# Exponential in PSUM, gate in the result copies, division at the end, three score units a pair, a new order

## The chip, the cores and the metric

The kernel runs on one core of a Trainium2 chip. Its engines work side by side, each through its own instructions in order, and wait for one another by semaphores: PE (TensorE, matrix products and transposes), DVE (VectorE), ACT (ScalarE), POOL (GpSimd) and SP (SyncE, which here only issues DMAs). SBUF is the working memory; PSUM takes what PE writes and can be read and written by DVE and ACT. The metric is the device time of one execution in microseconds.

## What is computed

Eight batches (`b`) of eight heads, 576 rows of 64. First a layer of attention: a causal softmax (`local`), and a linear memory that is read with a feature map `phi`; a gate `g` per head mixes both. Then a soft mixture of experts on the joined heads, with two softmaxes over the same logits: over all rows for each slot (dispatch `d`) and over the 32 slots for each row (combine `c`).

```
scores = q @ k.T / 8, causal;  a = exp(scores - max);  a /= a.sum + 1e-9;  local = a @ v
phi(x) = where(x > 0, x, exp(x) - 1) + 1
mem_out = (phi(q) @ M_prev) / (phi(q) @ z_prev + 1e-6)
x = g * mem_out + (1 - g) * local
logits = x @ moe_phi                                # 4608 rows x 32 slots
d = softmax over rows, c = softmax over slots
slot_in = d.T @ x;  slot_out[e] = relu(slot_in[e] @ w1[e]) @ w2[e];  out = c @ slot_out
```

## The kernel before, in words

**Attention part.** The 64 (batch, head) problems go two heads at a time: `n` counts 32 pairs. The first 64 rows of each head are taken out and done apart by the *aux* steps (names that begin with `a`, 16 units of two batches), so that a pair has 512 rows in four tiles `i` of 128, with 192, 320, 448 and 576 keys. For each pair the steps are, by the names of their functions `op_...`:

- `ldq`, `ldv` load. `qhi`, `qlo`, `khi`, `klo` split q and k into two parts (`X`, `K`); most of this is on POOL.
- `qp1` makes q + 1 on POOL (L375), `qexp` makes exp(q) on ACT (L379) into the SBUF tile `e`, and `qphi` joins them on DVE into `f` = max(min(e, 1), q + 1) (L383). `ap1`, `aexp`, `aphi` do the same for aux units (`af`, `ae`, `pha`, L537).
- `s` makes the scores in PSUM (L392, six matmuls for each stretch of keys), in four units: `3a` and `3b` (288 keys each of tile 3), `2` (448) and `10` (320 and 192). `mx` takes the mask and the running minimum of the negated scores on DVE (L416), and `ex` the exponential with its sum on ACT (L424), the sum going to the tile `sum`.
- `t` transposes the weights on PE (L427), `te` copies them out of PSUM (to `at`; L307 is the copy on ACT, L310 that on DVE), `av` multiplies with v (L455) into `oa`, `oe` copies the result to `os`.
- `rs` (L476) multiplies the sums with a gate factor into `R`. `u` brings `os` and the memory product into PSUM (L427, L489), `dn` (L493, L496) makes the reciprocals in `R`, `mu` (L501) multiplies all four parts by `R` into `w`, and `ad` adds the two halves on POOL (L514) into the batch tile `x`. For aux units `adn` (L596 to L598), `amu`, `aad` do the same.

For each of nine groups `g` (eight batches and the aux rows) follow `x3` (transpose x), `x1` (logits), `x1l` (copy them to `lt`), `x1m` (three DVE steps, L649 to L652: the group's maximum, the running maximum `mrun`, its negative `nmn`), `x1e` (exponentials), `x1d` (`den`, L663), `x2` and `x2m`, `x2e`, `x2s` (the softmax over slots; `row_scale`, L695 to L698, sums, adds 1e-9, inverts and multiplies), `x4` and `x4a` (L711, slot sums into `acc`).

**PSUM.** The pool `psD` has three slots of two banks (0, 1, 2); each unit (`s`, `t`, `u`, `x3` and others) takes one by a number written in the order. `psO` is one bank for `oa`. `psM` is one bank with a single buffer (`misc`): the aux values, the logits and the slot sums share it.

**Order.** Nothing is scheduled at run time. `SEQ` is one long table of steps, `step@n:slot`; the program emits them in this order, and each engine runs its own in that order. `EV` gives the engine of each copy (`a`, `p`, `v`). `w@x` are loads of expert weights, 512 KB each: 19 into tiles that stay, 18 more into tiles that attention no longer needs; `WORD` lists them.

**Tail.** After the last pair a few small steps (`y4` to `y12`) finish the dispatch softmax. Then the experts (`f1`, `f1t`, `f2`) run while the other 27 weight tiles are reloaded on SP's queue, and `comb` multiplies each group's `cT` with the experts' output; of its four 256-column results two are copied by ACT and two by DVE in one instruction each, and written out.

Of the kernel before, what the change touches and what calls it, by code (L numbers as in the profile page):

```python
# [26 lines left out]
gate@0 la@0 ldq@1 ldv@1 la@1 khi@0 qhi@0 qp1@0 qlo@0 qexp@0 klo@0 qphi@0 s.3a@0:0 ldq@2 s.2@0:1 aexp@0 ap1@0 mx.3a.0@0  # L27
mx.3a.1@0 s.3b@0:2 mx.2.0@0 as@0:0 mx.3b.0@0 ex.2.0@0 khi@1 mx.3b.1@0 ex.3.0@0 mx.2.1@0 klo@1 s.10@0:2 ex.3.1@0 aphi@0
amx.0@0 amx.1@0 mx.1.0@0 ex.2.1@0 t.A@0:0 qhi@1 mx.0.0@0 mx.1.1@0 aex.0@0 t.B@0:1 qlo@1 mx.0.1@0 te.A0@0 te.A1@0
aex.1@0 te.B0@0 te.B1@0 at@0:0 qp1@1 te.Bq@0 s.3a@1:2 ate@0 ex.1.0@0 s.2@1:0 khi@2 mx.3a.0@1 ex.0.0@0 mx.3a.1@1  # L30
s.3b@1:1 ex.1.1@0 mx.2.0@1 klo@2 s.10@1:2 ex.0.1@0 mx.3b.0@1 ex.2.0@1 av.3@0 rs@0 mx.3b.1@1 ex.3.0@1 qhi@2 mx.2.1@1
av.2@0 ex.3.1@1 qlo@2 mx.1.0@1 mx.0.0@1 aav@0 ex.2.1@1 mx.1.1@1 t.C@0:0 mx.0.1@1 ap1@1 aoe@0 oe.1@0 qexp@1 t.B@1:2
te.C0@0 te.C1@0 au@0:1 ldq@3 te.Cq@0 te.B0@1 te.B1@1 t.A@1:0 te.Bq@1 la@2 adn@0 ex.1.0@1 u.1@0:2 amu@0 te.A0@1 qphi@1
aad@0 s.3a@2:1 te.A1@1 av.0@0 dn.1@0 ex.0.0@1 av.1@0 mu.1@0 ex.1.1@1 av.3@1 mx.3a.0@2 ad.1@0 oe.0@0 mx.3a.1@2 ex.0.1@1
khi@3 aexp@1 av.2@1 rs@1 qexp@2 aphi@1 klo@3 aexp@2 u.0@0:1 oe.1@1 t.C@1:2 dn.0@0 ldv@2 qhi@3 s.3b@2:0 mu.0@0 te.C0@1
w@0 mx.3b.0@2 s.2@2:1 ad.0@0 te.C1@1 te.Cq@1 mx.3b.1@2 ex.3.0@2 as@1:2 qlo@3 mx.2.0@2 x3.0@0:0 ex.3.1@2 mx.2.1@2
# [1020 lines left out]
```

## Time and profile before

| | us |
|---|---|
| median of 3 runs | 500.87 (499.87 to 505.47) |
| profiled execution | 504.95 |
| its span, first to last instruction | 503.2 |
| PE busy | 413.8 (82%) |
| DVE busy | 369.2 (73%) |
| ACT busy | 320.1 (64%) |
| POOL busy | 205.9 (41%) |

The page shares out 503.2 us. A busy time is the time in which an engine had an instruction under way; PE's matmuls overlap, so its share is no measure of how near it is to its best. The attention part runs to about 420 us, the tail from 432 us on. TensorE's clock has two levels, and the profile gives the granted clock as a share of the upper one.

### The profile page before, as it was taken

To read this page: it belongs to the slowest core of one execution; us is meant where nothing else is said; L and a number is where in the kernel's file an instruction comes from. 1 tells how busy PE (TensorE), PEld (TensorE's weight loads), DVE (VectorE), ACT (ScalarE), POOL (GpSimd) and SP (SyncE) were. 2 spreads that over 40 slices of the span, in tenths; PEclk is the share of its full clock that TensorE was granted. 3 is DMA by queue.
4 is the path that set the end of the run, shared out by engine and by line. 5 is a ranking of instruction groups with operands and counts; after the bars stand their busy time and mean duration, and the time that the engine had idled before them with its cause. 6 is when DMAs were issued, how large, how long until landed. Compare 5 with 4: busy or idle time off the path is not lost. (4 is left out here: it accounts for less than half of the span.)

```text
span 503.2 us, 20521 instructions
## 1 busy us (share of the span) xinstructions
PE 413.8 (82%) x8597; PEld 336.5 (67%) x8597; DVE 369.2 (73%) x1301; ACT 320.1 (64%) x986; POOL 205.9 (41%) x259
## 2 busy tenths in 40 slices
...
GB/s 336 62 193 141 160 149 150 147 162 153 132 157 141 82 216 148 142 171 165 114 136 90 173 122 92 91 91 46 137 175 100 184 393 90 87 388 408 397 373 232
DMA packets 30940, 87.12 MB, mean 173 GB/s; under 512 B 2816, under 2 KB 12288, under 8 KB 30848
## 3 DMA queue, kind: packets, MB, share of 16 engines
...
q14 instruction: 24, 0.20, 0.1%
q10 hardware_dynamic: 288, 0.08, 0.1%
...
## 5 line engine op out<-in xcount | busy, mean ns | idle before, releaser
L424 ACT ACTIVATE p<-p,nm 128x192 f32<-128x192 f32 (+3 forms) x256 | 155.3, 610 | 23.0 <-DVE nm L416 22.8
L392 PE MATMUL psD<-K,X 64*128 64x288 f32 (+3 forms) x960 | 103.1, 335 | 28.0 <-DVE w L501 5.2
L416 DVE CUSTOM_DVE_ANT_0 p<-psD,mk 128x192 f32<-128x192 f32 (+3 forms) x256 | 109.8, 476 | 5.4 <-PE psD L392 5.3
L455 PE MATMUL oa<-at,vm 128*32 128x128 f32 (+1 forms) x3584 | 103.3, 267 | 2.5 <-ACT os L307 2.0
L455 PEld LDWEIGHTS oa<-at,vm 128*32 128x32 f32 x3584 | 93.6, 114 | 14.4 <-issue 8.6
L392 PEld LDWEIGHTS psD<-K,X 64*128 64x128 f32 x960 | 77.6, 194 | 38.3 <-issue 11.2
L307 ACT COPY at<-psD 128x512 f32<-128x512 f32 (+3 forms) x172 | 70.1, 444 | 49.6 <-DVE at L310 32.4
L514 POOL TENSOR_TENSOR x<-w 128x256 f32<-128x256 f32 x64 | 48.1, 751 | 103.8 <-DVE w L501 71.6
L427 PE MATMUL psD<-cs,p 64*128 64x64 f32 x1408 | 65.4, 227 | 11.7 <-DVE nm L416 4.2
L427 PEld LDWEIGHTS psD<-cs,p 64*128 64x128 f32 x1408 | 57.6, 142 | 17.8 <-ACT os L307 6.3
L310 DVE COPY at<-psD 128x512 f32<-128x512 f32 (+3 forms) x84 | 44.8, 545 | 23.4 <-ACT at L307 19.4
L424 ACT ACTIVATION_READ_ACCUMULATOR p<-p,nm 128x1 f32 x256 | 48.9, 191 | 0.0
L501 DVE TENSOR_TENSOR w<-psD,R 128x512 f32<-128x512 f32 x64 | 44.2, 691 | 4.2
L371 POOL TENSOR_TENSOR K<-qk,K 128x576 fp32r<-128x576 f32 x32 | 45.7, 1427 | 2.0 <-ACT K L307 0.4
L489 PE MATMUL psD<-vm,f 64*128 64x65 f32 x512 | 42.1, 278 | 1.0 <-issue 1.0
L363 POOL TENSOR_TENSOR X<-qk,X 128x512 fp32r<-128x512 f32 x31 | 39.7, 1279 | 2.5
L489 PEld LDWEIGHTS psD<-vm,f 64*128 64x128 f32 x512 | 36.9, 195 | 1.1 <-issue 1.1
L375 POOL TENSOR_SCALAR f<-qk 128x512 f32<-128x512 f32 x32 | 19.8, 620 | 33.1 <-PE psD L489 29.5
L383 DVE SCALAR_TENSOR_TENSOR f<-e,f 128x512 f32<-128x512 f32 x32 | 32.5, 1017 | 0.2 <-POOL f L375 0.2
L416 DVE CUSTOM_DVE_ANT_0 p<-psD,mk,nm 128x288 f32<-128x288 f32 x64 | 30.6, 509 | 0.6 <-PE psD L392 0.4
L312 POOL TENSOR_SCALAR K<-qk 128x576 fp32r<-128x576 f32 x31 | 21.5, 695 | 19.5 <-PE psD L392 18.0
L379 ACT ACTIVATE e<-qk 128x512 f32<-128x512 f32 x32 | 20.2, 632 | 9.8 <-DVE f L383 5.2
...
## 6 DMA issues: line engine op xcount, KB each, us to landing
...
```

The costliest lines, as they stand in the source:

```text
L307: nc.scalar.copy(o, i)
L310: nc.vector.tensor_copy(out=o, in_=i)
L363: ALU_ENG[ev("qlo", n)].tensor_tensor(out=x[:, 1], in0=st[n]["q"], in1=x[:, 0].bitcast(F32), op=ALU.subtract)
L371: ALU_ENG[ev("klo", n)].tensor_tensor(out=x[:, 1], in0=st[n]["k"], in1=x[:, 0].bitcast(F32), op=ALU.subtract)
L392: nc.tensor.matmul(ps[:, h, c:c + k1 - k0], s["X"][ROW[h], x, 128 * i:128 * i + 128], s["K"][ROW[h], y, o + k0:o + k1], start=(x, y) == (0 ...
L416: nc.vector.tensor_tensor_reduce(out=s["p", i][:, h, k0:k1], in0=s["s", u][:, h, c:c + k1 - k0], in1=maskq[:, o + k0:o + k1], op0=ALU.add, ...
L424: nc.scalar.activation(p, p, AF.Exp, scale=-1.0, bias=s["nm"][:, 2 * i + h:2 * i + h + 1], accum_out=s["sum"][:, i // 2, h, i % 2:i % 2 + 1])
L427: nc.tensor.transpose(out=o, in_=i, identity=ident[ROW[r], ROW[r]])
L455: nc.tensor.matmul(o[32 * j:32 * j + 32], w[:, 32 * j:32 * j + 32], rhs[j // 2], start=start, stop=stop)
L489: nc.tensor.matmul(ps[:, h, 65 * x:65 * x + 65], s["f"][ROW[h], 128 * i:128 * i + 128], s["m"][ROW[h]], start=True, stop=True)
L501: nc.vector.tensor_tensor(out=w, in0=s["u", u][:, :, 0:260].rearrange("a h (x d) -> a h x d", d=65)[:, :, :, 0:64], in1=s["R"][:, u].rearr ...
L514: ALU_ENG[ev(f"ad.{u}", n)].tensor_tensor(out=o, in0=w[:, :, 0:2], in1=w[:, :, 2:4], op=ALU.add)
```

## The change

Five edits, and with them a new `SEQ` and `EV`:

1. `qexp` and `aexp` write to the one bank `psM` instead of the SBUF tiles `e` and `ae`; the room freed in SBUF takes a twentieth resident weight tile.
2. The copies `oe` and `aoe` multiply by 1 - g, a column of one value per partition, so `rs` only adds 1e-9 and the sums of `ex` go straight into `R`.
3. `x1l` is gone. `slot_max` makes the negated logits `lt` and the running minimum in one DVE instruction that reads PSUM.
4. `x2s` only sums; the sums of all nine groups (`s36`) are inverted once, in the tail, and `comb`'s copies multiply by them. ACT does so in two instructions of 256 columns.
5. The score units are `3` (512 keys of tile 3), `2` (448 keys of tile 2, and the last 64 of tile 3) and `10`.

```diff
     def op_qexp(n):
-        st[n]["e"] = spl.tile([128, 512], F32, name="e")
+        st[n]["e"] = misc()
         nc.scalar.activation(st[n]["e"], st[n]["q"], AF.Exp)
...
-        for i, c, k0, k1 in {"3a": [(3, 0, 0, 288)], "3b": [(3, 0, 288, 576)], "2": [(2, 0, 0, 448)], "10": [(1, 0, 0, 320), (0, 320, 0, 192)]}[t]:
+        for i, c, k0, k1 in {"3": [(3, 0, 0, 512)], "2": [(2, 0, 0, 448), (3, 448, 512, 576)], "10": [(1, 0, 0, 320), (0, 320, 0, 192)]}[t]:
...
+    def act_scaled(o, i, c):
+        nc.scalar.activation(o, i, AF.Copy, scale=c)
+    def dve_scaled(o, i, c):
+        nc.vector.tensor_scalar(out=o, in0=i, scalar1=c, scalar2=None, op0=ALU.mult)
...
-        ENG[ev(f"oe.{u}", n)](s["os"][:, c], s["oa"][:, c])
+        SCALED[ev(f"oe.{u}", n)](s["os"][:, c], s["oa"][:, c], omg[:, n % NP:n % NP + 1])
     def op_rs(n):
-        nc.vector.scalar_tensor_tensor(out=s["R"][:, :, :, 2:4], in0=s["sum"], scalar=1e-9,
-                                       in1=omg[:, n % NP].rearrange("a (u h x) -> a u h x", u=2, h=2), op0=ALU.add, op1=ALU.mult)
+        r = st[n]["R"][:, :, :, 2:4]
+        nc.vector.tensor_scalar(out=r, in0=r, scalar1=1e-9, scalar2=None, op0=ALU.add)
...
     def op_aexp(n):
-        us[n]["e"] = spl.tile([128, 2, 64], F32, name="ae")
+        us[n]["e"] = misc()[:, 0:128].rearrange("a (m x) -> a m x", m=2)
...
-        nc.vector.scalar_tensor_tensor(out=R[:, :, 1], in0=s["sum"], scalar=1e-9, in1=gh[1], op0=ALU.add, op1=ALU.mult)
+        nc.vector.tensor_scalar(out=R[:, :, 1], in0=R[:, :, 1], scalar1=1e-9, scalar2=None, op0=ALU.add)
...
+    def slot_max(t, p1, old, new):
+        nc.vector.tensor_tensor_reduce(out=t, in0=p1, in1=maskq[:, 0:128], op0=ALU.add, op1=ALU.min, scale=-1.0, scalar=old, accum_out=new)
     def op_x1m(g):
-        mx = sml.tile([128, 1], F32, name="mx")
-        nc.vector.reduce_max(out=mx, in_=xs[g]["lt"], axis=AX.X)
-        nc.vector.tensor_tensor(out=mnew(g), in0=mold(g), in1=mx, op=ALU.max)
-        nmn = xs[g]["nmn"] = sml.tile([128, 1], F32, name="nmn")
-        nc.vector.tensor_scalar(out=nmn, in0=mnew(g), scalar1=-1.0, scalar2=None, op0=ALU.mult)
+        xs[g]["lt"] = sml.tile([128, 128], F32, name="lt", bufs=1)
+        slot_max(xs[g]["lt"], xs[g]["p1"][:, 0:128], mold(g), mnew(g))
...
-    def row_scale(c):
-        s4 = sml.tile([128, 4], F32, name="s4")
-        nc.vector.tensor_reduce(out=s4.rearrange("a (r j) -> a r j", r=2), in_=c, axis=AX.X, op=ALU.add)
-        nc.vector.tensor_scalar(out=s4, in0=s4, scalar1=1e-9, scalar2=None, op0=ALU.add)
-        nc.vector.reciprocal(out=s4, in_=s4)
-        nc.vector.tensor_tensor(out=c, in0=c, in1=four(s4), op=ALU.mult)
+    def row_sum(c, g):
+        nc.vector.tensor_reduce(out=s36[:, g], in_=c, axis=AX.X, op=ALU.add)
...
-            (act, dve)[half](o[:, 2 * half:2 * half + 2, :], ps[:, :, 0:256])
+            r = s36[:, g, half]
+            if half:
+                nc.vector.tensor_tensor(out=o[:, 2:4, :], in0=ps[:, :, 0:256], in1=r.rearrange("a (j o) -> a j o", o=1).broadcast_to([128, 2, 256]), op=ALU.mult)
+            else:
+                for v2 in range(2):
+                    act_scaled(o[:, v2, :], ps[:, v2, 0:256], r[:, v2:v2 + 1])
```

On DVE, around the slot softmax of the first batch. `f`, `den`, `R`, `os`, `m`, `c`, `at` and `s` are outputs of the steps named above; a number behind a name is the buffer's. Before:

```order
L652 TENSOR_SCALAR nmn<-mrun_65 128x1
L383 SCALAR_TENSOR_TENSOR f<-e,f 128x512
L663 SCALAR_TENSOR_TENSOR den<-den,al,sm 128x1
L476 SCALAR_TENSOR_TENSOR R<-sum,gt 128x4x2
L310 COPY os<-oa 128x256
L682 TENSOR_REDUCE m_1692<-psD_1657 128x4
L684 TENSOR_TENSOR c<-psD_1657,m_1692 128x128
L310 COPY at<-psD_1675 128x2x4x64
L695 TENSOR_REDUCE s_1716<-c 128x4
L696 TENSOR_SCALAR s_1716<-s_1716 128x4
L697 RECIPROCAL s_1716<-s_1716 128x4
L698 TENSOR_TENSOR c<-c,s_1716 128x128
```

The three small steps behind the sum `s` are gone in the changed kernel, `pha` reads PSUM (`psM`), and an aux unit's `aR` and a pair's `mu` stand in this place. DVE in the changed kernel, same batch:

```order
L597 TENSOR_SCALAR aR<-aR 128x2
L598 SCALAR_TENSOR_TENSOR aR<-psD_1441,gt 128x2
L600 RECIPROCAL aR<-aR 128x4
L605 TENSOR_TENSOR aw<-psD_1441,aR 128x256
L495 SCALAR_TENSOR_TENSOR R<-psD_1451,gt 128x2x2
L498 RECIPROCAL R<-R 128x8
L308 COPY at<-psD_1470 128x2x3x64
L683 TENSOR_REDUCE m_1506<-psD_1495 128x4
L685 TENSOR_TENSOR c<-psD_1495,m_1506 128x128
L503 TENSOR_TENSOR w<-psD_1451,R 128x512
L695 TENSOR_REDUCE s_66<-c 128x4
L539 SCALAR_TENSOR_TENSOR pha<-psM,af 128x2x64
```

On PE, the scores of the second pair; each `psD` number is one use of a slot. Before, four uses:

```order
L392 MATMUL psD_258<-K,X 128x288 x6
L392 MATMUL psD_268<-K,X 128x448 x6
L392 MATMUL psD_282<-K,X 128x288 x6
L392 MATMUL psD_293<-K,X 128x320 x6
L392 MATMUL psD_293<-K,X 128x192 x6
```

In the changed kernel three uses (204, 219, 283), with transposes of the first pair (L431) ahead of the third:

```order
L396 MATMUL psD_204<-K,X 128x512 x6
L396 MATMUL psD_219<-K,X 128x448 x6
L396 MATMUL psD_219<-K,X 128x64 x6
L431 MATMUL psD_236<-cs,p_188 128x64 x12
L431 MATMUL psD_236<-cs,p_161 128x64
L431 MATMUL psD_236<-cs,p_188 128x64
L431 MATMUL psD_257<-cs,p_161 128x64 x16
L396 MATMUL psD_283<-K,X 128x320 x6
L396 MATMUL psD_283<-K,X 128x192 x6
```

On ACT in the changed kernel, behind the first batch's slot exponentials (`ex`): the two exponentials into `psM` (L536 of an aux unit, L383 of a pair) stand in line with copies and score exponentials (L428).

```order
L652 ACTIVATE ex,sm<-lt,mrun_65 128x128
L654 ACTIVATE al<-mrun_64,mrun_65 128x1
L536 ACTIVATE psM<-au 128x128
L305 COPY at<-psD_1470 128x128
L305 COPY at<-psD_1470 128x2x3x64
L305 COPY ext<-psD_1495 128x128
L692 ACTIVATE c<-c 128x128
L305 COPY at<-psD_1510 128x2x4x64 x2
L383 ACTIVATE psM<-qk 128x512
L428 ACTIVATE p_1558,R<-p_1558,nm 128x192
```

What moved is that these two now need `psM` free before they start, and what follows them on ACT stands behind them.

## Rows read from the trace of the kernel before

**Rows 1.** Busy time by stretches: start:end, length, each engine (instructions), clock, DMA, GB/s.
```profile
13.50:27.00 13.50, 11.20 (x278) 10.04 (x282) 12.10 (x49) 12.37 (x43) 7.38 (x9) 1.00 0.21 73
135.00:148.50 13.50, 12.88 (x254) 11.64 (x252) 9.29 (x35) 8.41 (x27) 6.05 (x7) 0.76 0.27 86
378.00:391.50 13.50, 10.94 (x258) 8.95 (x246) 12.08 (x45) 9.73 (x32) 7.26 (x8) 1.00 0.36 125
```

**Rows 2.** Chain of waits, 245 to 419 us: by line; then start, us, what.
```profile
by line: DVE p L416 12.1%; PE oa L455 10.3%; ACT at L307 9.5%; ACT p L424 9.4%; DVE at L310 8.9%; PE psD L392 6.7%; PE psD L427 6.2%; issue 5.1%; DVE w L501 4.7%; DVE f L383 3.1%; PE psD L489 2.5%; PE psM L635 1.9%; ACT e L379 1.7%; DVE R L
...
286.02 0.60 DVE mrun L650
286.80 1.72 DVE f L383
```

**Rows 3.** Single lines: count, then least/median/greatest ns, first and last start.
```profile
L383 DVE SCALAR_TENSOR_TENSOR f<-e,f x32: 677/688/1799, 8.4 to 403.7; 128x512 f32<-128x512 f32 x32
L537 DVE SCALAR_TENSOR_TENSOR pha<-ae,af x16: 279/440/1352, 12.7 to 314.8; 128x128 f32<-128x128 f32 x16
L711 DVE SCALAR_TENSOR_TENSOR acc<-acc,al,psM x8: 733/738/747, 84.6 to 389.4; 128x512 f32<-128x512 f32 x8
L696 DVE TENSOR_SCALAR s<-s x9: 169/571/624, 82.5 to 444.7; 128x4 f32<-128x4 f32 x9
L596 DVE SCALAR_TENSOR_TENSOR aR<-asum,gt x16: 145/149/155, 23.0 to 328.4; 128x2 f32<-128x2 f32 x16
```

**Rows 4.** Groups by line and shape, DVE: count, busy us, mean ns, idle before.
```profile
L383 DVE SCALAR_TENSOR_TENSOR f<-e,f 128x512 f32<-128x512 f32 x32 | 32.5, 1017 | 0.2 <-POOL f L375 0.2
L476 DVE SCALAR_TENSOR_TENSOR R<-sum,gt 128x8 f32<-128x8 f32 x32 | 10.9, 342 | 4.2 <-ACT p L424 4.2
L537 DVE SCALAR_TENSOR_TENSOR pha<-ae,af 128x128 f32<-128x128 f32 x16 | 9.5, 597 | 0.1
L650 DVE TENSOR_TENSOR mrun<-mrun,mx 128x1 f32<-128x1 f32 x8 | 3.8, 473 | 0.3
L696 DVE TENSOR_SCALAR s<-s 128x4 f32<-128x4 f32 x9 | 3.7, 414 | 0.3
L698 DVE TENSOR_TENSOR c<-c,s 128x128 f32<-128x128 f32 x9 | 3.6, 404 | 0.3
L649 DVE TENSOR_REDUCE mx<-lt 128x1 f32<-128x128 f32 x8 | 2.3, 285 | 1.9 <-ACT lt L307 1.7
L697 DVE RECIPROCAL s<-s 128x4 f32<-128x4 f32 x9 | 1.6, 178 | 0.3
```

**Rows 5.** The same view, the score maxima on DVE.
```profile
L416 DVE CUSTOM_DVE_ANT_0 p<-psD,mk 128x448 f32<-128x448 f32 x64 | 37.9, 618 | 3.6 <-PE psD L392 3.6
L416 DVE CUSTOM_DVE_ANT_0 p<-psD,mk,nm 128x288 f32<-128x288 f32 x64 | 30.6, 509 | 0.6 <-PE psD L392 0.4
L416 DVE CUSTOM_DVE_ANT_0 p<-psD,mk 128x288 f32<-128x288 f32 x64 | 26.8, 451 | 0.5 <-PE psD L392 0.5
L416 DVE DVE_READ_ACCUMULATOR2_ANT nm<- 128x1 f32 x320 | 26.0, 81 | 0.0
```

**Rows 6.** The same view, ACT.
```profile
L307 ACT COPY os<-oa 128x256 f32<-128x256 f32 x46 | 16.5, 361 | 11.6 <-PE oa L455 9.5 <-PE oa L814 2.1
L307 ACT COPY w<-pp 128x512 f32<-128x512 f32 x10 | 5.8, 587 | 3.5 <-PE pp L952 3.5
L660 ACT ACTIVATE ex<-lt,nmn 128x128 f32<-128x128 f32 x8 | 3.1, 388 | 0.0
L691 ACT ACTIVATE c<-c 128x128 f32<-128x128 f32 x8 | 2.5, 313 | 2.4 <-DVE c L684 2.4
```

**Rows 7.** Waits: who waited for whom, us in total, times, longest.
```profile
PE psD L392 <- DVE w L501: 5.2, 14, 0.6
```

**Rows 8.** Busy time by stretches of 3 us in the tail, columns as in rows 1.
```profile
447.00:450.00 3.00, 3.00 (x32) 0.78 (x24) 0.54 (x1) 0.37 (x2) 0.00 (x0) 1.00 1.03 421
480.00:483.00 3.00, 2.56 (x26) 1.49 (x26) 2.10 (x4) 1.77 (x4) 0.00 (x0) 1.00 1.09 380
489.00:492.00 3.00, 0.00 (x0) 0.00 (x0) 0.00 (x0) 0.00 (x0) 0.00 (x0) 0.58 1.04 354
```

More of the change, by code (lines that the diff above doesn't have):

```diff
@@ L26 @@
 SEQ = """
[L27 to L36, printed above, removed]
@@ L329, in setup @@
         nc.sync.dma_start(out=cs, in_=cst[:, 0:256])
-        nc.scalar.dma_start(out=gc, in_=beta)
+        nc.scalar.dma_start(out=gt[:, :, 0:5], in_=beta)
         nc.scalar.dma_start(out=ph, in_=phi)
-        nc.scalar.activation(gc, gc, AF.Exp, scale=-1.0)
+        nc.scalar.activation(gt[:, :, 0:5], gt[:, :, 0:5], AF.Exp, scale=-1.0)
         nc.vector.memset(one, 1.0)
@@ L420, in op_ex @@
         s, i, h = st[n], int(i), int(h)
-        if "sum" not in s:
-            s["sum"] = sml.tile([128, 2, 2, 2], F32, name="sum")
+        if "R" not in s:
+            s["R"] = sml.tile([128, 2, 2, 4], F32, name="R")
         p = s["p", i][:, h]
-        nc.scalar.activation(p, p, AF.Exp, scale=-1.0, bias=s["nm"][:, 2 * i + h:2 * i + h + 1], accum_out=s["sum"][:, i // 2, h, i % 2:i % 2 + 1])
+        nc.scalar.activation(p, p, AF.Exp, scale=-1.0, bias=s["nm"][:, 2 * i + h:2 * i + h + 1], accum_out=s["R"][:, i // 2, h, 2 + i % 2:3 + i % 2])
     def turn(o, i, r):
@@ L555, in op_aex @@
         s, h = us[n], int(h)
-        if "sum" not in s:
-            s["sum"] = sml.tile([128, 2], F32, name="asum")
-        nc.scalar.activation(s["p"][:, h], s["p"][:, h], AF.Exp, scale=-1.0, bias=s["nm"][:, h:h + 1], accum_out=s["sum"][:, h:h + 1])
+        if "R" not in s:
+            s["R"] = sml.tile([128, 2, 2], F32, name="aR")
+        nc.scalar.activation(s["p"][:, h], s["p"][:, h], AF.Exp, scale=-1.0, bias=s["nm"][:, h:h + 1], accum_out=s["R"][:, h, 1:2])
     def op_at(n):
@@ L798, in op_y8n @@
     def op_y8n(_):
-        nc.vector.tensor_scalar(out=ngm, in0=y["pm"][:, 128:129], scalar1=-1.0, scalar2=None, op0=ALU.mult)
+        dve(ngm, y["pm"][:, 128:129])
     def op_y8a(_):
-        nc.scalar.activation(ag, mrun[1], AF.Exp, bias=ngm)
+        nc.scalar.activation(ag, mrun[1], AF.Exp, scale=-1.0, bias=ngm)
     def op_y8e(_):
@@ L842, in op_y11 @@
     def op_y11(_):
-        nc.vector.scalar_tensor_tensor(out=den, in0=den, scalar=y["al"], in1=y["sm"], op0=ALU.mult, op1=ALU.add)
-        nc.vector.tensor_tensor(out=den, in0=den, in1=ag, op=ALU.mult)
+        nc.vector.tensor_scalar(out=den, in0=den, scalar1=y["al"], scalar2=y["sm"], op0=ALU.mult, op1=ALU.add)
+        nc.vector.tensor_scalar(out=den, in0=den, scalar1=ag, scalar2=None, op0=ALU.mult)
     def op_y12(_):
```

501 lines of the change are left out of this document (249 added, 252 removed).

## Prediction

> **What bounds the kernel now.** I read the busy times by stretches first, 13.5 us each. The 30 stretches from 13.5 to 418.5 us are the attention part. In 16 of them DVE is the busiest of PE and DVE; [rows 1] has the first and the last of these (DVE 12.10 and 12.08 of 13.5, PE 11.20 and 10.94, ACT 12.37 and 9.73). In the other 14 PE leads, most clearly at 135 us, where the granted clock averages 0.76 between its levels of 1.2 and 2.4 GHz: PE 12.88, DVE 9.29. So DVE is the first bound of about half of the attention part, with PE and ACT close behind.
>
> Next the chain of waits from 245 to 419 us: its first line is a sum by line, and the feature map's combination on DVE (`f`, L383) holds 3.1% of these 174 us, 5.4 us [rows 2]. One of its pieces takes 1.72 us at 286.8, shortly behind an instruction on `mrun`, 128 x 1, that takes 0.60.
>
> Then least, median and greatest duration of single lines [rows 3]. `f` takes 677 ns at least and 1799 at most; the aux heads' `pha` 279 to 1352. Both read only SBUF. The accumulation into `acc`, the same instruction over 512 columns but with an operand from PSUM, always takes 733 to 747. A DVE instruction here is slow when all its tensors are in SBUF, and POOL, which works in SBUF alone, is busy 6 to 7.4 us of these stretches [rows 1]; I take that for a wait for POOL. The means hold these waits: 1017, 597, 473, 414, 404 ns [rows 4].
>
> **The change part by part, on DVE.** The exponential goes to PSUM, so `f` and `pha` read one tensor from SBUF and one from PSUM. For `f` the bounds are 677 (its own least) and 738 (median of `acc`, which also carries a pointer scalar); I take 720, nearer `acc` because that one reads PSUM. 32 x (1017 - 720) = 9.5 us go, 8.9 to 10.9 by the bounds. For `pha` I take 279 + 61 = 340, the 61 being 738 - 677: 16 x (597 - 340) = 4.1 us.
>
> The slot maximum becomes one instruction that reads PSUM. The score maxima price it: 618 ns at 448 columns and 451 at 288 give 1.04 ns a column, so 285 at 128; a start value by pointer adds 509 - 451 = 58, the accumulator's read 81 [rows 5]: 424 ns. It replaces a reduction (285) and the `mrun` step (473) [rows 4], and a third small one that I leave out: 8 groups x 334 ns = 2.7 us.
>
> The combine's division leaves each group: 414 + 178 + 404 ns [rows 4], 8 groups inside attention, 8.0 us. Its sum stays.
>
> The result copies now carry the gate as a pointer scalar. 23 are on DVE: 23 x 58 ns = 1.3 us more. Counted in the order, DVE also takes over 13 copies and 256 columns net from ACT: 13 x 151 ns (451 - 288 x 1.04) + 256 x 1.04 = 2.2 us more. `rs` (342 ns mean [rows 4]) remains an instruction on SBUF alone, in place, and I leave its price.
>
> The score maxima: 288 + 288 columns cost 451 + 509 = 960 ns, 512 + 64 cost 685 + 276 = 961 by the same slope. Nothing; nor for PE, whose 30 matmuls and 1536 columns a pair stay (a 64-column one might not hide its weight load; DVE's lead covers that in 16 stretches, and it is in the upper end).
>
> DVE's sum: 9.5 + 4.1 + 2.7 + 8.0 - 1.3 - 2.2 = 20.8 us less.
>
> **On ACT.** 57 result copies (361 ns now for 256 columns) get a pointer. An activation with pointer and accumulator takes 388, one with neither 313 [rows 6], so at most 75 ns each, 4.3 us; it loses the copy of the slot scores and the 13 copies. About even, and hidden by ACT's idle time of 3.8 us in the last stretch of [rows 1]; without that cover it is 4.3 us. In "ScalarE: Activation LUTs", What ACT_TABLE_LOAD costs, the Trainium skill charges a pointer operand about 93 ns, which speaks against this step: by it an estimated 5.3 us in place of 4.3.
>
> **Slots.** A pair takes three score units in place of four, 32 fewer of 391 uses of the three double banks. Score matmuls waited 14 times, 5.2 us in all, until DVE's last reader had freed a slot [rows 7]. A quarter of 128 score units goes, so 1.3 us; the bounds are 0 and 5.2.
>
> **How much of it becomes time.** 20.8 us over 30 stretches are 0.7 each. Where DVE leads, that brings it just to PE: in the first stretch of [rows 1] 12.10 falls to 11.4, PE stands at 11.2. Where PE leads, nothing comes back. So 16/30 of 20.8, 11.1 us, and 1.3 for the slots.
>
> **The tail.** One more weight tile stays resident, so 26 reloads of 512 KB follow the attention part in place of 27. They run with the DMA queues full, 1.03 and 421 GB/s [rows 8]: 0.524 MB / 421 GB/s = 1.25 us. The final copies get dearer on ACT, two of 256 columns with a pointer for one of 512: 2 x (361 + 75) - 587 = 285 ns, 18 times, 5.1 us [rows 6]. At 480 us ACT is busy 1.77 of 3, so this fits, and at 489 no engine works any more while DMA stands at 1.04 [rows 8]: the writes cover it. Were they not the end, up to 5.1 us would come back.
>
> Sum: 11.1 + 1.3 + 1.25 = 13.7 us. The profiled execution took 504.95, of which 503.2 span: 491.3. It lies 4.1 us above the median of 500.87, so I put the median of the changed kernel at 487.
>
> **Rivals.** *All of DVE's gain counts*, if PE's waits were DVE's too, so that the pair's period shrinks with DVE: 20.8 + 2.5 = 23.3, 478 us. For it: the chain between 245 and 419 us lists DVE's lines first. Against: PE's 12.88 of 13.5 with DVE idle a third.
>
> *The next engine takes over at once.* PE and the ACT copies replace DVE in the chain (ACT's `at` and `p` hold 9.5% and 9.4% of it [rows 2]); then only slots and tail remain, and perhaps 1 or 2 us more: 497.
>
> *The waits move over.* POOL does as much as before, so an SBUF-only instruction that is left can meet it. `aR` of the aux heads took 145 to 155 ns, never with a wait, while `s`, as small, took 169 to 624 [rows 3]; `aR` becomes a tensor_scalar on SBUF, as `s` is. At the mean of `s` 16 x (414 - 149) = 4.2 us return to DVE, 16/30 of it 2.3: 490. The Trainium skill ("SBUF — State Buffer", Who interferes with whom) says that a tensor_scalar on SBUF can take a mode of two ports and then contends with GpSimd, and that a DVE instruction with at most one SBUF input outside these modes does not. By that rule `f` and `pha` are free of waits and `aR` and `rs` are not; the trace agrees for `s`.
>
> *Slower: the one miscellaneous bank.* `psM` has one buffer. Up to now 36 uses share it (aux values, slot logits, slot sums), with the 48 exponentials 84. An exponential must wait for the bank's last reader, and ACT's copies and score exponentials stand behind it in order. Each holds the bank from its own start until DVE has combined, `f`'s 720 ns included. If each of the 48 waits 0.29 us on the path, that eats 13.7 us and the gain is gone; at 0.45 us, 21.6 in all, the kernel is 8 us slower, 509. For it: in the order an aux exponential may stand several copies ahead of the use. Against: most `qphi` follow their `qexp` within a third of a pair's steps, so the bank is mostly held briefly.
>
> **How the numbers follow.** Forecast 0.40 (487, from 482 to 492), waits move over 0.12 (490), all counts 0.20 (478), next engine 0.18 (497), one bank 0.10 (509). About a third of the next-engine case is still over 1% faster; 1% is what a measurement of this kernel can tell from no change, 496 to 506 us here. Faster 0.40 + 0.12 + 0.20 + 0.05 = 0.77, the same 0.13, slower 0.10. The range leaves out the one-bank case and the far end of "all counts": 475 to 500.
>
> **What would show it.** `f` at about 720 ns with a greatest value close to its least, `pha` about 340; DVE some 20 us less busy; no `s` lines in the groups but one; 26 reloads. The attention part ending 12 us earlier. Wrong if ACT waits in front of the exponentials for DVE's readers of `psM`, if PE's waits grow by as much as DVE's work shrinks, or if `f` keeps its spread.

## Result and profile after

The changed kernel takes 468.47 us (median of 4 runs, 461.54 to 471.39), the kernel before, beside it, 501.64 (499.87 to 505.47). The ratio is 0.9247, with a 95% interval of 0.9113 to 0.9381; on another chip it was 0.9204 (0.9132 to 0.9275). The ratio leaves out the slower executions (here 469.76 and the profiled 471.39 of the changed kernel), so it is not the quotient of the two medians. So it is some 8% faster, 38 to 40 us, where 13.7 had been forecast. The 468 lies below the range of 475 to 500.

The profiled execution took 471.39 us, of which 469.6 span. A second profile, e13 in the table below, has a span of 465.9 and gives the same readings to 5 us. First the page's busy times by engine of after; before had PE 413.8, DVE 369.2, ACT 320.1 and POOL 205.9 us.

```profile
PE 415.2 (88%) x8597; PEld 340.6 (73%) x8597; DVE 342.6 (73%) x1278; ACT 323.0 (69%) x984; POOL 199.7 (43%) x258
```

VectorE is busy 26.6 us less, not 20.8. Its instructions overlap: added up group by group its work fell from 435.2 to 414.8, by 20.4. TensorE's work is the same to 1.4 us, and its share of the span rose from 82 to 88%: it stood idle less. The waits view of PE shows that, summed over all its rows: 71.5 us before (43.9 of them until VectorE, 23.2 until ScalarE), 41.5 after (19.1 and 16.4).

Least, median and greatest duration of single lines of after, which answer to [rows 3]:

```profile
L387 DVE SCALAR_TENSOR_TENSOR f<-psM,f x32: 674/682/693, 10.0 to 377.5; 128x512 f32<-128x512 f32 x32
L539 DVE SCALAR_TENSOR_TENSOR pha<-psM,af x16: 275/281/292, 25.5 to 305.7; 128x128 f32<-128x128 f32 x16
L479 DVE TENSOR_SCALAR R<-R x32: 148/208/1395, 25.4 to 382.9; 128x8 f32<-128x8 f32 x32
L597 DVE TENSOR_SCALAR aR<-aR x16: 117/162/1257, 34.1 to 315.2; 128x2 f32<-128x2 f32 x16
```

`f` and `pha` have lost their spread. `aR`, 145 to 155 ns before, now has one.

Groups by line and shape of after: the score maxima, the slot maximum, the copies with a pointer on VectorE and ScalarE, and the two that stayed in SBUF (count, busy us, mean ns, idle before). They answer to [rows 4 to 6].

```profile
L420 DVE CUSTOM_DVE_ANT_0 p<-psD,mk 128x512 f32<-128x512 f32 x64 | 42.5, 682 | 3.6 <-PE psD L396 3.5
L420 DVE CUSTOM_DVE_ANT_0 p<-psD,mk,nm 128x64 f32<-128x64 f32 x64 | 16.8, 275 | 1.3 <-PE psD L396 1.3
L314 DVE TENSOR_SCALAR os<-oa,gt 128x256 f32<-128x256 f32 x19 | 9.1, 478 | 2.8 <-PE oa L459 1.9 <-ACT os L311 0.8
L647 DVE CUSTOM_DVE_ANT_0 lt<-psM,mk,mrun 128x128 f32<-128x128 f32 x9 | 3.1, 340 | 2.9 <-PE psM L637 2.9
L479 DVE TENSOR_SCALAR R<-R 128x8 f32<-128x8 f32 x32 | 13.2, 413 | 1.3 <-ACT p L428 1.3
L597 DVE TENSOR_SCALAR aR<-aR 128x2 f32<-128x2 f32 x16 | 5.4, 338 | 0.0
...
L311 ACT ACTIVATE os<-oa,gt 128x256 f32<-128x256 f32 x45 | 20.9, 468 | 13.1 <-PE oa L459 12.3 <-DVE os L314 0.5
L311 ACT ACTIVATE w<-pp,s 128x256 f32<-128x256 f32 x18 | 7.4, 472 | 3.7 <-PE pp L940 3.4
```

Where the stretches changed: two of after, with the columns of [rows 1].

```profile
13.50:27.00 13.50, 12.16 (x188) 11.34 (x190) 9.42 (x43) 9.07 (x30) 4.77 (x7) 0.56 0.02 8
135.00:148.50 13.50, 12.43 (x262) 10.46 (x259) 11.31 (x45) 10.62 (x35) 3.08 (x6) 1.00 0.37 124
```

The stretch at 135 us, which ran at a mean clock of 0.76 before, has 1.00 and more instructions of all three engines (262 matmuls for 254), though not the same part of the work. The first one has 0.56, a mean of the two levels: most of it, at the start of the program, ran at 1.2 GHz.

The attention part is where the gain lies. The last `w<-psD,R` of the span starts at 390.8 us, at 419.3 before, so 28.5 us go there and 5.1 of the span behind it (83.9 to 78.8).

### The profile page after: what moved, and what is told of

Same layout as the page of the kernel before. It is cut to its first block, busy times and chain, and to the rows that moved or that the text cites. A ratio compares the mean times of both kernels' runs of the same rounds, so it can differ in the third digit from the quotient of the medians.

```text
span 469.6 us, 20484 instructions
## 1 busy us (share of the span) xinstructions
PE 415.2 (88%) x8597; PEld 340.6 (73%) x8597; DVE 342.6 (73%) x1278; ACT 323.0 (69%) x984; POOL 199.7 (43%) x258
## 4 chain that ended last, share of the span: by engine, by line
PE 40%; ACT 22%; DVE 20%; DMA 9%; issue 4%; POOL 2%; POOLq 0%; SPq 0%; ACTq 0%; DVEq 0%
PE oa L459 12%; ACT p L428 9%; PE psD L396 9%; PE psD L431 8%; ACT at L305 8%; DVE p L420 6%; DVE at L308 5%; DMA w<-in_w_dram 4%; PE pp L940 2%; DMA qk<-in_w_dram 2%; PE psD L491 2%; ACT os L311 2%; DVE w L503 2%; DMA qk<-in_qk_dram 1%; DMA gt<-in_beta_dram 1%
## 5 line engine op out<-in xcount | busy, mean ns | idle before, releaser
L428 ACT ACTIVATE p<-p,nm 128x576 f32<-128x576 f32 (+3 forms) x256 | 155.5, 612 | 16.3 <-DVE nm L420 15.4
L420 DVE CUSTOM_DVE_ANT_0 p<-psD,mk 128x512 f32<-128x512 f32 (+3 forms) x256 | 126.5, 533 | 8.8 <-PE psD L396 8.3
L396 PE MATMUL psD<-K,X 64*128 64x64 f32 (+4 forms) x960 | 100.6, 341 | 9.6 <-ACT psM L383 2.4
L459 PE MATMUL oa<-at,vm 128*32 128x128 f32 (+1 forms) x3584 | 105.3, 266 | 1.6 <-ACT os L311 0.6
L396 PEld LDWEIGHTS psD<-K,X 64*128 64x128 f32 x960 | 81.0, 194 | 17.7 <-ACT psM L383 3.2
L431 PE MATMUL psD<-cs,p 64*128 64x64 f32 x1408 | 68.0, 232 | 9.6 <-DVE at L308 2.7
L431 PEld LDWEIGHTS psD<-cs,p 64*128 64x128 f32 x1408 | 58.2, 144 | 18.0 <-DVE at L308 3.5
L428 ACT ACTIVATION_READ_ACCUMULATOR p<-p,nm 128x1 f32 x256 | 49.4, 193 | 0.0
L316 POOL TENSOR_SCALAR X<-qk 128x512 fp32r<-128x512 f32 x30 | 18.6, 619 | 53.4 <-DMA qk<-in_qk_dram 27.6
L311 ACT ACTIVATE os<-oa,gt 128x256 f32<-128x256 f32 x45 | 20.9, 468 | 13.1 <-PE oa L459 12.3
L431 PE MATMUL psD<-cs,os 64*128 64x64 f32 x256 | 22.2, 236 | 5.8 <-ACT at L305 1.7
L420 DVE DVE_READ_ACCUMULATOR2_ANT nm<- 128x1 f32 x320 | 26.5, 83 | 0.0
```

The source lines that it names most:

```text
L396: nc.tensor.matmul(ps[:, h, c:c + k1 - k0], s["X"][ROW[h], x, 128 * i:128 * i + 128], s["K"][ROW[h], y, o + k0:o + k1], start=(x, y) == (0 ...
L420: nc.vector.tensor_tensor_reduce(out=s["p", i][:, h, k0:k1], in0=s["s", u][:, h, c:c + k1 - k0], in1=maskq[:, o + k0:o + k1], op0=ALU.add, ...
L428: nc.scalar.activation(p, p, AF.Exp, scale=-1.0, bias=s["nm"][:, 2 * i + h:2 * i + h + 1], accum_out=s["R"][:, i // 2, h, 2 + i % 2:3 + i ...
L431: nc.tensor.transpose(out=o, in_=i, identity=ident[ROW[r], ROW[r]])
L459: nc.tensor.matmul(o[32 * j:32 * j + 32], w[:, 32 * j:32 * j + 32], rhs[j // 2], start=start, stop=stop)
```

## Experiments

Each run has its own ratio to the kernel before on the same chip; a gain is told in per cent of that, 1% being 5 us. Two theories to begin with: A, VectorE's relief carries the gain and all of it becomes time; B, the new order and its three units carry it. One table first, of profiled executions. PE idle and DVE idle are sums over all rows of the waits view of that engine.

| kernel | ratio | span us | mean clock | PE busy | PE idle (until DVE, ACT) | DVE busy | DVE idle |
|---|---|---|---|---|---|---|---|
| before | 1 | 503.2 | 0.939 | 413.8 | 71.5 (43.9, 23.2) | 369.2 | 107.8 |
| e9 old order, rest of the new arithmetic | 0.9805 | 495.1 | 0.939 | 412.7 | 65.3 (35.1, 24.9) | 361.8 | 110.4 |
| e10 old order, exponentials in PSUM | 0.9948 | 502.2 | 0.947 | 413.3 | 72.3 (45.8, 20.2) | 355.9 | 120.7 |
| e5 old order, three units | 1.0489 | 529.0 | 0.916 | 432.4 | 80.0 (43.0, 29.8) | 364.2 | 140.3 |
| e1 new order with three units, old arithmetic | 0.9565 | 482.2 | 0.947 | 411.1 | 54.9 (29.5, 14.9) | 358.8 | 101.1 |
| after, second profile (e13) | 0.9204 | 465.9 | 0.954 | 409.3 | 40.4 (18.3, 14.6) | 343.3 | 102.4 |
| e14 after, exponentials close behind maxima | 0.9813 | 490.6 | 0.939 | 416.7 | 58.6 (18.0, 37.6) | 340.0 | 131.3 |
| e12 after without the additions of 1e-9 | 0.9123 | 457.7 | 0.962 | 404.5 | 38.8 (14.4, 17.3) | 329.4 | 108.4 |

Read it along PE: its busy time plus its idle time follows the span (from e1 to e13 16.3 us less span, 1.8 less busy, 14.5 less idle). The matmuls are the same 8597 in every row, and PE's busy time follows the granted clock, to some 4 us: at 0.939 it is 412.7, 413.8 and 416.7.

Where PE's idle time went shows in the group of the score matmuls: before, e5, e1 and the second profile of after.

```profile
L392 PE MATMUL psD<-K,X 64*128 64x288 f32 (+3 forms) x960 | 103.1, 335 | 28.0 <-DVE w L501 5.2
L389 PE MATMUL psD<-K,X 64*128 64x512 f32 (+4 forms) x960 | 103.7, 348 | 27.8 <-DVE w L498 6.2
L391 PE MATMUL psD<-K,X 64*128 64x64 f32 (+4 forms) x960 | 98.0, 334 | 9.3 <-DVE K L309 1.8
L396 PE MATMUL psD<-K,X 64*128 64x64 f32 (+4 forms) x960 | 101.2, 342 | 8.4 <-DVE nm L420 2.4
```

The new order with its three units takes 19 us of idle time from in front of the scores (28.0 to 9.3), whatever the arithmetic; three units in the old order take nothing (27.8). In front of the transposes the rows of the waits view add up to 30.3 us in before, 30.8 in e1, 20.8 in e13: there the new arithmetic gains.

**Order or arithmetic?** e1 takes the arithmetic of before into the new order; in one of the nine groups the weights are transposed ahead of their scaling there, so that group's output isn't scaled, while every instruction runs.

```diff
-gate@0 la@0 ldq@1 ldv@1 la@1 khi@0 qhi@0 qp1@0 qlo@0 qexp@0 ... s.3a@0:0 ldq@2 s.2@0:1
+gate@0 ldq@1 la@0 la@1 ldv@1 qhi@0 khi@0 qp1@0 klo@0 qlo@0 qexp@0 ... s.3a@0:0 ldq@2 s.2@0:1
-"3a": [(3, 0, 0, 288)], "3b": [(3, 0, 288, 576)], "2": [(2, 0, 0, 448)]
+"3": [(3, 0, 0, 512)], "2": [(2, 0, 0, 448), (3, 448, 512, 576)]
```

> The old arithmetic (exponentials in SBUF, gate in the factors R, a weight scaled in every group, 19 resident weights) in the new order with three score units per pair. Theory A (VectorE's relief carries the gain, and converts fully because TensorE was no second bound): order and units give little, 493 to 505 us, ratio 0.98 to 1.00 of before. Theory B (the new order and its fewer PSUM slots carry it): 470 to 480 us, ratio 0.94 to 0.96.

482.63 us, ratio 0.9565 (0.9471 to 0.966). Theory B: the order with its units alone brings 4.4%, more than the whole forecast. Part of that is VectorE's own waits. Groups of e1, in which these instructions are those of before:

```profile
L382 DVE SCALAR_TENSOR_TENSOR f<-e,f 128x512 f32<-128x512 f32 x32 | 25.5, 798 | 0.5 <-ACT e L378 0.3
L536 DVE SCALAR_TENSOR_TENSOR pha<-ae,af 128x128 f32<-128x128 f32 x16 | 5.8, 364 | 1.0 <-ACT ae L533 0.9
L595 DVE SCALAR_TENSOR_TENSOR aR<-asum,gt 128x2 f32<-128x2 f32 x16 | 5.0, 310 | 0.0
```

`f` fell from 1017 to 798 ns and `pha` from 597 to 364 [rows 4] with both operands in SBUF; `aR` rose from 149 to 310. So how long these waits for POOL last depends on the order and not on the operands alone.

The other way round, e2 is the arithmetic of after, with its three units, in the order of before.

> The new arithmetic with its three score units in the order of before: steps stand where they stood, only the exponentials into PSUM move (behind the last user of their bank) and s.3b falls away. Theory A: 468 to 478 us, ratio 0.93 to 0.95. Theory B: 485 to 497 us, ratio 0.97 to 0.99, with the feature map's exponential now waiting for the one bank of psM.

530.14 us, ratio 1.0501 (1.0389 to 1.0612): slower than before, which neither theory had. Two suspects came with it: the exponentials that hold the bank of psM, and the three units. e6 shortens the hold:

```diff
-... qexp@17 ... (up to 66 steps) ... qphi@17
+... qexp@17 ... (6 steps or fewer) ... qphi@17
```

> The new arithmetic in the order of before once more, as in the run at 530 us, but the exponential is issued at most 6 steps ahead of the maximum that reads it, instead of up to 66, so that it holds the one bank of psM for a short time. Theory hold (the 27 us lost there were the users of psM that waited behind a bank held for nothing): 488 to 495 us, as the price list of the prediction would have it. Theory that the old order suits the new arithmetic in no form: over 510 us.

526.69 us, 1.0433 (1.0363 to 1.0503): about 3 us less, with intervals that overlap, so the hold is not what costs 25. e5 has the units and nothing else (but for six slot numbers and a few neighbouring steps):

```diff
-... s.3b@16:1 amu@9 te.C0@15 aphi@10 s.2@16:2 aad@9 mx.3b.0@16 te.C1@15 ...
+... amu@9 te.C0@15 aphi@10 s.2@16:2 aad@9 mx.3b.0@16 te.C1@15 ...
```

> Before, with its arithmetic and its order, but three score units per pair (s.3b falls away, its last 64 columns ride in unit 2's tile): 359 PSUM tiles instead of 391. The 20 us that the order of after with its three units brought to the old arithmetic (ratio 0.9565) are either the units' or the order's. Theory units: 482 to 488 us. Theory order: 497 to 503 us (the prediction's term for the units was 1.3 us, bounds 0 to 5.2).

529.76 us, 1.0489 (1.0392 to 1.0586). The step that saves 32 uses of the PSUM banks costs 25 us in an order that was made for four. Waits of e5, of which before had 22.8 (28 times) for `p <- nm` and 5.7 (14 times) for `p <- psD`:

```profile
ACT p L421 <- DVE nm L413: 39.6, 38, 2.4
...
DVE p L413 <- PE psD L389: 23.7, 24, 2.6
```

VectorE waits for score matmuls and ScalarE for maxima. Of the 25.8 us of span only 8.5 are new idle time of PE; 18.6 are PE's busy time at the same 8597 matmuls. Two stretches of e5, columns of [rows 1]:

```profile
81.00:94.50 13.50, 11.65 (x214) 9.25 (x203) 10.09 (x34) 8.41 (x28) 2.83 (x6) 0.75 0.28 98
162.00:175.50 13.50, 11.72 (x200) 10.18 (x202) 9.21 (x32) 8.28 (x27) 2.17 (x4) 0.75 0.34 123
```

A mean of 0.75 is half of the stretch at 1.2 GHz: 200 matmuls are busy for 11.72 us where before had 278 in 11.20 [rows 1], if of another mix. So the loss shows twice: as idle time, and as slower matmuls. Which of the two costs the time and which only fills it isn't shown.

**What is the order worth, then?** From e5 to e1 only the order (and the table of the copies' engines) changes: 1.0489 to 0.9565, 46 us. e8 takes that table back, in after:

```diff
-EV = (the table of after: which engine makes which copy)
+EV = (the table of before)
```

> After with the table of before that says which engine makes which copy (the steps stand as in after). If the gain of the new order lies in the copies' engines: 476 to 488 us. If it lies in the order of the steps: 466 to 473 us.

475.57 us, 0.9424 (0.9357 to 0.9491): in after about 2%, 10 us, hang on who copies. If it is no more between e5 and e1, most of the 46 us hangs on where the steps stand. No run has the new order with four units, so what the units are worth in it is open.

Counted over 24 pairs in the middle of the two orders, and told as means for each kind of step, a maximum stands 4 to 9 steps ahead of its exponential in before and 7 to 18 in after (the median over all is 6 against 7.5: it is the long ones that grew), the last exponential 9 to 12 ahead of the transposes that read it against 16 to 19, and a pair runs over 152 steps against 170 from its first scores to its last `ad`. But the last reader of a PSUM slot stands 7.0 steps ahead of the score unit that takes the slot in before and 6.2 in after, so distance doesn't explain why the scores wait less, nor why the transposes of e1, at the distances of after, wait as long as in before.

e14 takes the first of these distances away in after: 204 of its 256 score exponentials move, so that all stand 2 to 7 steps behind their maxima (in before 2 to 36), and the sums get a third buffer. e15 moves the maxima `mx.3b` of every pair 8 steps later in e5. Of each the place of one pair:

```diff
 e14: mx.2.1@16 te.Cq@15 te.C1@15 av.3@15 mx.3b.0@16 ex.2.1@16 mx.2.0@16 ex.3.0@16 av.0@15 mx.3b.1@16 qphi@16
-av.1@15 ex.2.0@16 oe.1@15 at@9:0 x3.2@3:1 rs@15 ex.3.1@16
+ex.2.0@16 av.1@15 oe.1@15 ex.3.1@16 at@9:0 x3.2@3:1 rs@15
 e15:
-s.2@16:2 aad@9 mx.3b.0@16 te.C1@15 te.Cq@15 mx.3b.1@16 ex.3.0@16 w@14 u.1@15:0 mx.2.0@16
+s.2@16:2 aad@9 te.C1@15 te.Cq@15 w@14 u.1@15:0 mx.2.0@16 as@10:1 mx.3b.0@16 mx.2.1@16 av.0@15 mx.3b.1@16 ex.3.0@16
```

> After with each exponential of the scores at most 4 steps behind the maximum that it waits for, as in before, instead of 7 to 18 (204 of 256 moved; the sums get a third buffer). All else stands as in after. Theory distance (the new order gains because nothing is asked for right behind the step that makes it): ScalarE waits for VectorE's maxima again, 478 to 495 us, ratio 0.945 to 0.98. Theory that ScalarE's place doesn't matter and TensorE's sequence alone does: 464 to 472 us, ratio 0.92 to 0.93.

494.27 us, 0.9813 (0.9724 to 0.9902): 28 to 31 us lost. Waits of e14, where after has 5.4, 1.0, 23.1 and 13.0 (e13):

```profile
PE psD L431 <- ACT at L305: 11.0, 16, 2.0
PE psD L431 <- ACT os L311: 10.0, 14, 1.9
...
DVE at L308 <- ACT at L305: 38.8, 42, 2.7
ACT p L428 <- DVE nm L420: 20.4, 25, 3.0
```

ScalarE itself waits only 7 us longer for maxima. What grew is what waits for ScalarE: its copies stand behind exponentials that stand still, and the transposes need the banks that those copies empty (PE's idle time until ScalarE 14.6 to 37.6; in front of the transposes 20.8 to 36.9, in front of the scores only 8.4 to 11.1). That an order made for its own durations loses by any large move is not excluded: no run moves as many steps and keeps the distance.

> The run with three units in the old order (529.8 us), with the maxima mx.3b 8 steps later, so 12 steps behind unit 2 as in after, and their exponentials behind them. Theory distance (mx.3b stood right behind a unit that has twelve matmuls now instead of six, and VectorE and then ScalarE wait there): 508 to 520 us. Theory that something else in the three units costs (tiles held longer, a larger first maximum): 525 to 533 us.

541.34 us, 1.0723 (1.0652 to 1.0795): 12 us worse than e5, not better. The waits of e15:

```profile
ACT p L421 <- DVE nm L413: 56.7, 45, 2.7
...
DVE p L413 <- PE psD L389: 23.6, 27, 1.8
```

VectorE's wait for the unit did not move (23.7 to 23.6), so standing right behind the unit was not its cause, and ScalarE's grew. A later maximum also pushed the exponentials of tile 3 towards the transposes (6 steps where there had been 12), and PE's idle time in front of the transposes rose from 35.2 to 47.8. So the run says little about distance in such an order, and what exactly makes three units so dear in it stays open.

**How much of an engine's work becomes time?** The prediction took 16 of 30. e3 and e4 double one instruction group in before, e16 and e17 the same in after.

```diff
+        for _ in range(2 if (t, h) == ("2", 0) else 1):          # e3, e17: mx.2.0 twice
+            for _ in range(2 if (t, i) == ("2", 2) else 1):      # e4, e16: unit 2 twice
```

> Before with one score maximum (mx.2.0, 448 columns, 617 ns and the 80 ns read of its minimum) run twice in each of 32 pairs: 22.3 us more on VectorE. The prediction's conversion (VectorE leads in 16 of 30 stretches) means +12 us, about 513. If VectorE is the bound all through, +20 to +24 us, 521 to 525. If neither engine is a bound, but the waits between them, under +10 us.

> Before with the six matmuls of score unit 2 (448 columns) run twice in each pair: 32 x about 0.68 us from start to start = 21.8 us more on TensorE. If TensorE is the next bound close behind VectorE, as the prediction has it (it leads in 14 of 30 stretches): +10 us or more, about 512. If its busy time overstates it and it has room: +5 us or less, under 507.

e3: 518.08 us, 1.029 (1.0207 to 1.0373), 15 us, 0.65 of the work added. e4: 513.08 us, 1.0196 (1.0089 to 1.0303), 10 us, 0.45. So in before both count about half, near the forecast's factor; which counts more the intervals don't tell (10 to 19 us for e3, 4 to 15 for e4). PE's busy time in e4 by the page:

```profile
PE 426.8 (84%) x8789; PEld 351.0 (69%) x8789; DVE 371.1 (73%) x1301; ACT 322.0 (63%) x986; POOL 205.7 (40%) x259
```

It rose by 13.0 us for 21.8 added. The mean clock rose with it, from 0.939 to 0.959, but that isn't all: in e16, at 0.954 like e13, it rose by 16.0 (409.3 to 425.3).

> After with the six matmuls of 448 columns of score unit 2 run twice in each pair, 21.8 us more on TensorE, as was done to before, where it cost 0.45 of that. If TensorE is now the bound: 0.7 to 1.0 of it, 15 to 22 us over after, ratio 0.95 to 0.965. If the conversion is as before: 10 us, ratio 0.94.

> After with the maximum mx.2.0 run twice in each pair, 22.3 us more on VectorE, as was done to before, where it cost 0.65 of that. If VectorE no longer leads: 0.2 to 0.4 of it, 4 to 9 us over after, ratio 0.93 to 0.94. If the conversion is as before: 14 us, ratio 0.95.

e16: 478.50 us, 0.9455 (0.9369 to 0.9541). e17: 480.67 us, 0.9452 (0.9322 to 0.9583). Against 0.9204 and 0.9247 for after that is 10 to 13 us each, 0.5 to 0.6 of what was added. Work counts about as it did in before: no engine alone bounds after, as none bounded before.

**The parts of the arithmetic in the old order.** Both have the four units of before. e9 has the gate in the copies, the slot maximum and the late division, in the order of before less `x1l`. e10 has only the exponentials in PSUM; to free the bank it also moves each `qexp` up to its `qphi`, from 23 to 100 steps apart to 2 to 7.

```diff
 e9, against after, beside the order, the units and the copies' table:
-        st[n]["e"] = misc()
+        st[n]["e"] = spl.tile([128, 512], F32, name="e")
 e10, against before, beside the moved exponentials:
-        st[n]["e"] = spl.tile([128, 512], F32, name="e")
+        st[n]["e"] = misc()
```

> The order, the four score units and the SBUF exponentials of before, with the rest of the new arithmetic: gate in the copies, slot maximum in one instruction, weights divided at the end (19 resident weights). VectorE loses 8.0 us (row_scale) and 2.7 us (slot maximum) and gains 1.3 us. Theory of the prediction (0.53 to 0.65 of it counts, with 1 us at the end): ratio 0.985 to 0.990, 496 to 500 us. Theory that in the old order VectorE's relief is lost in other waits (with three units in that order 16.5 us less of VectorE were worth 3 us): ratio 0.995 to 1.00.

497.23 us, 0.9805 (0.9724 to 0.9886): 10 us, with an interval of 6 to 14, where the forecast had 5 for this part. Two groups of e9, in which both instructions are a tensor_scalar on SBUF as in after:

```profile
L482 DVE TENSOR_SCALAR R<-R 128x8 f32<-128x8 f32 x32 | 17.2, 536 | 5.4 <-ACT p L431 5.4
L600 DVE TENSOR_SCALAR aR<-aR 128x2 f32<-128x2 f32 x16 | 2.5, 159 | 0.0
```

In the old order `rs` rises from 342 to 536 ns with its new form, `aR` hardly (149 to 159).

> Before with its order and four score units; only the two exponentials go into the bank of psM, issued at most 6 steps ahead of the maximum that reads them. Theory of the prediction (f 9.5 us and pha 4.1 us of VectorE, 0.53 to 0.65 of it counts): 7 to 9 us faster, ratio 0.982 to 0.986. Theory that the one bank costs as much as the wait for POOL did: ratio 0.995 to 1.01.

503.63 us, 0.9948 (0.9907 to 0.999): 2.6 us, a third of the forecast. The groups and waits of e10:

```profile
L383 DVE SCALAR_TENSOR_TENSOR f<-psM,f 128x512 f32<-128x512 f32 x32 | 22.0, 688 | 3.5 <-ACT psM L379 2.8 <-POOL xa L610 0.5 <-POOL f L375 0.2
L476 DVE SCALAR_TENSOR_TENSOR R<-sum,gt 128x8 f32<-128x8 f32 x32 | 10.3, 322 | 7.6 <-ACT p L424 7.6
...
PEld psM L455 <- DVE f L383: 10.0, 11, 1.6
PE psM L455 <- DVE f L383: 8.3, 9, 1.4
```

`f` is down to 688 ns. But VectorE, 13.3 us less busy, is 12.9 us more idle: among others it waits for ScalarE's exponentials in front of `f` (2.8, before none) and of `R` (7.6, before 4.2 [rows 4]). And TensorE's matmuls into psM now wait until `f` has read the bank. So the time of the waits for POOL came back as idle time. How much of that the moved `qexp` brought, and how much the bank, no run separates.

In the new order the same part was undone in after (e7).

```diff
-        st[n]["e"] = misc()
+        st[n]["e"] = spl.tile([128, 512], F32, name="e")
```

> After with both exponentials back in SBUF (tiles e and ae; the 20th resident weight gives up its room, so 27 reloads instead of 26, about 1 us). Theory of the prediction (f 9.5 us and pha 4.1 us of VectorE, the largest term): at 0.53 to 0.65 of time for one of VectorE 7 to 9 us more, 476 to 480 with the reload. Theory that the new order had already taken most of that wait away (the run with the old arithmetic in the new order shows f at 798 ns and pha at 364 ns): 32 x 114 + 16 x 82 ns = 5.0 us of VectorE, 3 us, 472 to 474 with the reload.

472.44 us, 0.9364 (0.9297 to 0.9431), against 0.9204 and 0.9247: 6 to 8 us by the ratios, with intervals that overlap; but the last `w` starts at 389.8 us in its profile, at 390.8 and 386.4 in the two of after. What the bank is worth in the new order, between nothing and 8 us, is not settled.

**After without the additions of 1e-9.** Each sum of a score softmax holds the exponential of 0, so it is at least 1 and 1e-9 changes nothing in float32. e12 leaves that addition out.

```diff
-        nc.vector.tensor_scalar(out=r, in0=r, scalar1=1e-9, scalar2=None, op0=ALU.add)
-        nc.vector.tensor_scalar(out=R[:, :, 1], in0=R[:, :, 1], scalar1=1e-9, scalar2=None, op0=ALU.add)
```

> After without the additions of 1e-9 to the sums of the score softmax (rs and the first instruction of adn): every sum holds an exponential of 0 and is at least 1, so in float32 the addition changes nothing. It takes 32 x 413 + 16 x 338 ns = 18.6 us from VectorE, the two instructions that came to wait for POOL. If VectorE's relief counts by 0.65: 12 us faster than after, ratio about 0.90 of before. If it counts as little as the exponentials in PSUM did in this order (5 us of VectorE for 1 to 4 us): 2 to 8 us faster, 0.91 to 0.92.

> After, unchanged, beside the three above on one chip: 464 to 472 us, ratio 0.92 to 0.935; its first 30 us tell whether the granted clock of 0.56 between 13.5 and 27 us is the program's or that execution's.

e12: 461.14 us, 0.9123 (0.9042 to 0.9204); after beside it 465.78, 0.9204 (0.9132 to 0.9275). Some 4 us, for 13.9 us less VectorE work (343.3 to 329.4): 0.3 of it. The second profile of after has 0.63 between 13.5 and 27 us, so a low clock there was not one execution's alone. e18 and e19, also without the additions, try the start.

```diff
-gate@0 ldq@1 la@0 ...                # the gate first in SEQ, its exponential in setup()
+... gate@0 av.2@0 ...                # e18, e19: both behind the first pair's transposes
-WARM = 3
+WARM = 5                             # e19 only
```

> After without the additions of 1e-9, and with the gate's exponential and its three VectorE instructions behind the first pair's transposes instead of first in their queues (there ScalarE waits until 6 to 7 us for a small load). 0 to 3 us under the run without the additions (ratio 0.912), the mask's load at 7.8 us being next: 0.905 to 0.912 of before.

> The same with 5 instead of 3 warming matmuls on TensorE, which end at about 8 us, where the scores begin. If the half clock in the first 27 us comes from TensorE's idle time between warm-up and scores: a granted clock of 1.00 there in the profiled run and 0 to 4 us less. If not: no difference, or the first scores start later.

458.71 us, 0.9133 (0.907 to 0.9196), and 459.32, 0.915 (0.9091 to 0.9208): no different from e12. With the longer warm-up the profile shows a clock of 1.00 in the stretch that has 0.67 in e18, yet the time is the same. So the additions of 1e-9 are what counts: three kernels without them stand at 0.912 to 0.915, after at 0.920 and 0.925. That is 8.5 to 9% under before; against after it is about 1%, with intervals that still overlap.

## Why the prediction was wrong

**What held.** `f` came to 684 ns on the mean (720 taken, 677 to 738 as bounds) and its spread is gone; `pha` to 282 (340). The slot maximum takes 340 + 82 ns (424 foretold). The score maxima take 682 + 275 ns instead of 960. A pointer on VectorE's copies costs 60 ns (418 to 478; 58 foretold). So the prices on VectorE were right to some 5%, but for `pha`, which came 17% under. The pointer on ScalarE was not: 361 to 468 (ACTIVATE in place of COPY), 107 ns and not 75.

**"How much of it becomes time: 16 of 30."** As a factor for work added to before it was fair (0.65 and 0.45 measured). The step that failed is to use it for each term. In the order of before, 13.6 us priced for `f` and `pha` gave 2.6, not 7.3: VectorE's idle time grew by about what its busy time lost (e10). 9.4 us for the slot maximum, the division and the gate gave 10, not 5, though VectorE was only 7.4 less busy (e9). If the two add up, which no run tests, these errors cancel by luck: 12.6 us, where the forecast had 12.4 for VectorE's relief and the slots.

**The moved order had no term.** This is the step by which the number was missed. The prediction read the order of after only for counts (13 copies, 2.2 us) and for the distance of `qphi`, and kept the waits of before for everything else. The new order with its three units, with the arithmetic of before, is worth 22 us (e1), and makes the new arithmetic worth 16 to 18 us in it (0.9565 to 0.9204 or 0.9247) instead of 12, though e1's own interval is 5 us to each side. Its first effect is on waits of which the prediction priced one row: PE's idle time in front of the score matmuls, 28.0 us to 9.3. "What bounds the kernel" had the sign of this: both engines led in turn, none full, so much of the loss lay in waits between them, 71.5 us of idle PE, that an order can take away.

**"Slots: 1.3 us, bounds 0 and 5.2."** Wrong by itself, in sign: 25 us slower in the order of before. The upper bound was misread too: 5.2 us is one row of the view, the wait for `w` alone, of 28.0 in front of the score matmuls. Three units left these at 27.8 in the old order and brought new waits: VectorE's for scores 5.7 to 23.7, ScalarE's for maxima 22.8 to 39.6.

**The tail.** 1.25 us were foretold. The run with 27 reloads in the new order (e7) has 80.3 us behind the start of the last `w`, after 78.8 and, in its second profile, 79.5: 0.8 to 1.5 us for the reload. The other 3.6 us (83.9 to 80.3) were not followed up. The copies with a pointer (2 x 472 - 587 = 357 ns, 18 times) are hidden: the span behind that `w` got no longer.

**The rivals.** *All of the gain counts* (478) came nearest, but not by its mechanism, since 0.5 to 0.65 of doubled work counts. *The next engine takes over at once* is refuted by the same runs: VectorE's work still counts by half in after (e17). *The waits move over* has its mechanism: `aR` from 149 to 338 ns and `rs` from 342 to 413, 16 x 189 + 32 x 71 = 5.3 us back on VectorE (4.2 foretold for `aR`). The Trainium skill ("SBUF — State Buffer", Who interferes with whom) says that a tensor_scalar on SBUF can contend with GpSimd; the traces agree, down to 128 x 2 elements: 117 ns at least and 1257 at most. But for `aR` it is the place in the order that brought the wait: as a tensor_scalar in the old order it takes 159 ns (e9), as before's scalar_tensor_tensor in the new one 310 (e1). `rs` has it with its new form in the old order too (536 ns in e9). *The one bank* is real in the old order (8.3 us of PE's matmuls in e10), and small in the new one: the waits view of after has no row in which a matmul into psM waits for `f` or `pha`, and ScalarE's exponentials wait 2.3 us for the bank's readers (`pha` 1.4, `acc` 0.9).

**The part of the clock.** The prediction's sum has no term for it. PE's busy time for the same number of matmuls runs from 404.5 (e12, clock 0.962) to 435.4 us (e2, 0.912); of the 25.8 us that e5 loses 18.6 lie there. Whether this time is lost by the clock, or the clock was low where PE had time to spare, isn't settled; in e19 the better clock at the start gained nothing.
